# More unused transposes ahead of the first matrix unit of a planned attention and feed-forward kernel

## The chip, the cores and the metric

The kernel runs on one core of a Trainium2 chip. Its engines work side by side, each through its own list of instructions in order: TensorE (PE: matmuls, and PEld: the loads of their weights), VectorE (DVE), ScalarE (ACT), GpSimd (POOL), and SyncE (SP), whose list here holds the DMA issues. [...] The metric is the device time of one execution in microseconds (us); lower is better. The number given for a kernel is the median of its runs.

## The reference

Two blocks follow each other. The first is a causal linear attention with decay, in 4 batches x 8 heads, 768 tokens, 64 values per head; the second is a feed-forward block over the resulting 3072 x 512 matrix.

```python
for b in range(nb):                      # blocks of 64 tokens
    intra = np.einsum('bhic,bhjc->bhij', qb, kb) * Dmask[None]
    intra = np.einsum('bhij,bhjd->bhid', intra, vb)
    inter = np.einsum('bhid,bhde->bhie', qb * lam_pow[None], kv_state)
    out[:, :, sl] = intra + inter
    kv_state = lam_block * kv_state + np.einsum('bhsd,bhse->bhde', kb * rev_pow[None], vb)
x = out.transpose(0, 2, 1, 3).reshape(3072, 512)
h = x @ w_in                             # 512 x 2048, given as float64
result = np.maximum(0.01 * h, h) @ w_out # 2048 x 512, given as float64
```

## The kernel before

**Attention.** Tokens go in 24 chunks of 128 (two blocks of 64, all 8 heads at once). For a chunk c, SP loads k, q and v (`load_kq`, L338, two halves of four heads each; `load_v`, L388). PE transposes k and q in four steps each (`transposes`, L403, one pair of steps per half load), ACT copies the transposed tiles out of PSUM (L414 for k, L415 for q). PE multiplies in `scores` (L313, into the PSUM tile psc): the scores of the chunk, and the new part of the state from k and v. The k used for the state has been scaled by its decay on POOL (L419; on DVE in chunk 0), and q by its own (L423). DVE masks the scores (L452, giving "sc") and adds the state (L459); POOL decays the state (L462). `outputs` forms the chunk's output on PE (L313, into po): own, from sc and v, then the part that comes from the state, in two halves with a small copy (L491) between them. ACT and DVE split the output in three parts xh, xl, xm (L507, L508, L510), which the feed-forward block multiplies separately.

**Feed-forward block.** A group is four chunks, 512 tokens. A unit (`up`, L640) multiplies a group by 256 columns of w_in, in three products (xh with wh, xl with wl, xm with wm). The weights come as float64 (load L566), are turned into float32 by ACT and DVE (L578 to L585) and split in three (L591 or L593, L596, L602). The first unit needs chunks 0 to 3. Once all ups are through, `down` (L700) multiplies by w_out.

**The plan.** Nothing above is emitted directly. Class `Plan` collects every piece of work with an estimated duration on its engine (`add`), what it reads and writes, and a rank. `emit` runs a simple model of the engines, always taking the piece that can start earliest, and so gets an order in time, `timeline`. The instructions are then emitted in that order. While it emits, `emit` runs a second estimate: `soon` holds when each engine will be free and `over` when each piece ends; the start of a piece is the larger of the two, with an allowance per engine (`LAG`, and for a load the one in `SOON`) between a producer and its user. This second estimate serves one end only: where PE would be idle for more than 0.4 us, `self.idle(n)` puts in n unused transposes first. That is `busy` (L266): it transposes the identity into the PSUM tile b10. No one reads the result, and the transposes wait for nothing but the identity. Eleven of them (`WARM`) stand at the head of PE's list. From the first piece that writes b10 (the first unit) on, `idle` is None and no more are put in.

The prologue on PE therefore reads: eleven unused transposes, k0 and q0 (transposes of chunk 0), scores and state of chunk 0, k1, own0, q1, rest of the outputs of 0, scores of 1, q2, own1, k2, rest of 1, scores of 2, q3, k3, own2, q4, rest of 2, scores of 3, own3, q5, rest of 3, first unit, with unused transposes at nine places between.

Of the kernel before, what the change touches and what calls it, by code (L numbers as in the profile page):

```python
# [33 lines left out]
    return bass.AP(ap.tensor, ap.offset, a[:idx] + [[0, n]] + a[idx:])  # L34


class Plan:

    LAG = {"PE": 0.25, "ACT": 0.1, "DVE": 0.1, "POOL": 0.12, "DMA": 3.5}
    SOON = dict(LAG, DMA=2.0)

    def __init__(self):
        self.ops, self.last, self.rank = [], {}, 0.0
# [36 lines left out]
    def emit(self):  # L83
        n = len(self.ops)
        follows, heads = {}, {}
        for c in self.chains.values():
            m = [i for i in c if "PE" in self.ops[i][0]]
            for i in c[1:]:
                self.ops[m[0]][2].update(self.ops[i][2] - set(c))
            heads[m[0]] = m[1:]  # L90
            follows.update((i, m[0]) for i in m[1:])
        locked = []
        left = [len(o[2]) for o in self.ops]
        users = [[] for _ in range(n)]
        for i, o in enumerate(self.ops):
            for d in o[2]:
                users[d].append(i)
        free = dict(self.first)
        ends = [[] for _ in range(n)]
        able = {e: set() for e in free}  # L100
        for i, o in enumerate(self.ops):
            if not left[i]:
                for e in o[0]:
                    able[e].add(i)

        def since(i, e):
            return max((t + (0.0 if e == x != "DMA" else self.LAG[x]) for t, x in ends[i]), default=0.0)

        def good(i, e, t):
            ways = self.ops[i][0]  # L110
            return all(t + ways[e] <= max(free[x], t) + ways[x] + 0.3 for x in ways)

        done = []
        while len(done) < n:
            best = None
            for e in free:
                for i in able[e]:
                    if e == "PE" and (i != locked[0] if locked else i in follows):
                        continue
                    t = max(free[e], since(i, e))  # L120
                    if (best is None or (t, self.ops[i][3]) < best[:2]) and good(i, e, t):
                        best = (t, self.ops[i][3], i, e)
            t, _, i, e = best
            ways, fn = self.ops[i][:2]
            if i in heads:
                locked = list(heads[i])
            elif locked and i == locked[0]:
                locked.pop(0)
            for x in ways:
                able[x].discard(i)  # L130
            us = ways[e]
            if e == "PE" and t < self.cold:
                us *= 1.5
            elif e == "DVE" and fn is not None and free["POOL"] > t:
                us += 0.4 * min(free["POOL"] - t, us)
            free[e] = t + us
            done.append((t, len(done), i, e))
            for u in users[i]:
                ends[u].append((free[e] + self.more.get(i, 0.0), e))
                left[u] -= 1  # L140
                if not left[u]:
                    for x in self.ops[u][0]:
                        able[x].add(u)
        self.timeline = sorted(done)

        soon = dict.fromkeys(free, 0.0)
        soon.update(PE=self.warm, DVE=self.first["DVE"], DMA=self.first["DMA"])
        over = [(0.0, None)] * n
        for t, _, i, e in self.timeline:
            ways, fn, deps = self.ops[i][:3]  # L150
            t = max([soon[e]] + [over[d][0] + (0.0 if over[d][1] == e != "DMA" else self.SOON[over[d][1]]) for d in deps])
            if e == "PE":
                if self.spare in self.ops[i][4]:
                    self.idle = None
                if self.idle is not None and t > soon[e] + 0.4:
                    self.idle(int((t - soon[e] - 0.2) / 0.22))
            soon[e] = t + ways[e]
            over[i] = (soon[e], e)
            fn() if len(ways) == 1 else fn(e)
# [661 lines left out]
```

## Time and profile before

| | us |
|---|---|
| median of 3 runs | 610.2 (609.88 to 610.89) |
| the profiled execution | 609.84 |
| its span | 608.1 |
| PE busy | 597.1 (98%) |
| DVE busy | 313.2 (52%) |
| ACT busy | 267.9 (44%) |
| POOL busy | 85.6 (14%) |
| first unit starts (L640) | 30.98 |
| unused transposes (L266) | 35 in all, first at 1.4, last at 29.5 |

All times of the profile count from the start of the span. A row of the timeline gives the start, how long the group lasts, engine, line, operation, output tile and input tile, shape, and the number of instructions; in brackets stands how long the engine was idle ahead of it and what ended that idle time. In a row of the table of waits come the total, the number and the longest of the waits. Starts of PE and PEld differ little; PEld is the sharper of the two for short groups, since ends of matmuls are modelled. The line of tenths splits the span in 40 slices of 15.2 us.

### The profile page before, as it was taken

How to read it: one execution, taken by the hardware profiler on the slowest of the kernel's cores; microseconds unless marked ns; L12 is line 12 of the kernel's file. 1: busy time of each engine (PE TensorE's matmuls, PEld its weight loads, DVE VectorE, ACT ScalarE, POOL GpSimd, SP SyncE). 2: the span in 40 equal slices, each digit the busy share in tenths (PEclk: the TensorE clock that was granted, in tenths of full speed). 3: DMA queues.
4: the chain of work that ended last, by engine and by line, in shares of the span. 5: the costliest groups of instructions: out<-in, count | busy, mean ns of one | idle time of the engine just before them, and what ended most of it. 6: DMA issues, size and time to landing. Idle time of an engine off the chain costs nothing.

```text
span 608.1 us, 12940 instructions
## 1 busy us (share of the span) xinstructions
PE 597.1 (98%) x5391; PEld 494.0 (81%) x5391; DVE 313.2 (52%) x417; ACT 267.9 (44%) x428; POOL 85.6 (14%) x91
## 2 busy tenths in 40 slices
PE   8799999999999999999999999999999999999997
PEld 6578888888888888888788888888888888888886
DVE  5899872334253426226366755545454544635531
ACT  4778874333455656565577422222222313214111
POOL 1653331215133014104000000000000000000000
PEclk9999999999999999999999999999999999999999
DMA  9899864767788888886686843424334343433201
GB/s 218 214 281 256 244 182 119 180 143 186 188 219 243 215 239 200 226 249 215 227 288 232 279 141 106 171 74 143 131 103 138 109 136 109 134 104 123 85 1 69
DMA packets 147754, 105.18 MB, mean 173 GB/s; under 512 B 123632, under 2 KB 124400, under 8 KB 147696
## 3 DMA queue, kind: packets, MB, share of 16 engines
q1 hardware_dynamic: 147552, 104.36, 58.9%
q8 instruction: 42, 0.69, 0.5%
q14 instruction: 16, 0.13, 0.1%
q10 hardware_dynamic: 144, 0.00, 0.0%
HBM read 68.69 MB, written 35.65 MB: 172 GB/s over the span
## 4 chain that ended last, share of the span: by engine, by line
PE 94%; DMA 2%; SPq 1%; ACT 1%; DVE 1%; issue 0%; DVEq 0%; ACTq 0%
PE b L640 44%; PE b L700 18%; PE po L700 11%; PE psc L700 11%; PE po L313 4%; PE pt L700 4%; PE psc L313 3%; DMA raw<-in_moe_w_in_dram 2%; SPq L338 1%; PE po L403 0%; PE pt L403 0%; ACT low L580 0%; DVE w L584 0%; DVE w L585 0%; SPq L388 0%
## 5 line engine op out<-in xcount | busy, mean ns | idle before, releaser
L682 ACT ACTIVATE xh<-att 128x1024 fp32r<-128x1024 f32 x48 | 50.7, 1060 | 148.9 <-PE b L700 140.7
L683 DVE SCALAR_TENSOR_TENSOR xl<-att,xh 128x1024 fp32r<-128x1024 f32 x48 | 58.6, 1222 | 95.6 <-ACT xh L682 95.6
L640 PE MATMUL b<-xh,wh 128*128 128x512 f32 (+1 forms) x392 | 102.9, 386 | 0.7 <-ACT xh L507 0.7
L640 PE MATMUL b<-xm,wm 128*128 128x512 f32 (+1 forms) x392 | 103.5, 391 | 0.0
L640 PE MATMUL b<-xl,wl 128*128 128x512 f32 (+1 forms) x392 | 102.8, 386 | 0.0
L640 PEld LDWEIGHTS b<-xh,wh 128*128 128x128 f32 x392 | 72.5, 188 | 15.8 <-ACT xh L507 0.9
L640 PEld LDWEIGHTS b<-xl,wl 128*128 128x128 f32 x392 | 72.5, 188 | 14.8
L658 ACT ACTIVATE b<-b 128x512 f32<-128x512 f32 x96 | 56.0, 584 | 63.1 <-PE b L640 63.1
L640 PEld LDWEIGHTS b<-xm,wm 128*128 128x128 f32 x392 | 70.9, 188 | 15.2 <-ACT b L658 0.7
L661 ACT ACTIVATE gs<-b 128x512 f32<-128x512 f32 x96 | 56.7, 598 | 42.2 <-PE b L640 37.7
L700 PE MATMUL b<-wh,xh 128*128 128x512 f32 x192 | 74.7, 389 | 0.0
L700 PE MATMUL b<-wl,xl 128*128 128x512 f32 x192 | 74.7, 389 | 0.0
L685 DVE SCALAR_TENSOR_TENSOR xm<-xl,xh 128x1024 fp32r<-128x1024 f32 x48 | 58.7, 1226 | 4.7
L700 PEld LDWEIGHTS b<-wl,xl 128*128 128x128 f32 x192 | 36.1, 188 | 7.6
L700 PEld LDWEIGHTS b<-wh,xh 128*128 128x128 f32 x192 | 36.0, 187 | 7.5
L452 DVE TENSOR_TENSOR att<-psc,att 128x512 f32<-128x512 f32 x24 | 16.5, 689 | 45.7 <-PE psc L313 45.7
L423 POOL TENSOR_TENSOR att<-att 128x512 f32<-128x512 f32 (+1 forms) x21 | 26.3, 1251 | 96.9 <-DVE att L383 42.5
L419 POOL TENSOR_TENSOR att<-att 128x512 f32<-128x512 f32 (+1 forms) x23 | 28.5, 1239 | 65.3 <-DMA att<-in_k_dram 19.9
L700 PE MATMUL psc<-wh,xh 128*128 128x512 f32 x96 | 37.3, 389 | 0.0
L700 PE MATMUL psc<-wl,xl 128*128 128x512 f32 x96 | 37.3, 389 | 0.0
L700 PE MATMUL psc<-wm,xm 128*128 128x512 f32 x96 | 37.3, 389 | 0.0
L700 PE MATMUL po<-wh,xh 128*128 128x512 f32 x96 | 37.3, 389 | 0.0
(73 smaller groups left out, 790.0 us busy)
## 6 DMA issues: line engine op xcount, KB each, us to landing
att<-g SPq DMA_DIRECT2D x48, 512.0 KB, 3.3
g<-gs SPq DMA_DIRECT2D x47, 512.0 KB, 4.0
raw<-in_moe_w_in_dram SPq DMA_DIRECT2D x16, 512.0 KB, 5.6
raw<-in_moe_w_out_dram SPq DMA_DIRECT2D x16, 512.0 KB, 4.7
att<-in_k_dram SPq DMA_DIRECT2D x48, 128.0 KB, 4.1
att<-in_v_dram SPq DMA_DIRECT2D x24, 256.0 KB, 4.3
out_dram<-gs SPq DMA_DIRECT2D x23, 256.0 KB, 2.1
wo<-w SPq DMA_DIRECT2D x8, 512.0 KB, 5.7
```

Of the source, the lines that this page charges most:

```text
L313: nc.tensor.matmul(dst[HALF[cols]], lhsT=lhsT[HALF[rows]], rhs=rhs[HALF[rows]], start=start, stop=True, skip_group_check=True)
L338: nc.sync.dma_start(out=dst[:, z * HP:(z + 1) * HP, :], in_=y[z::2].rearrange("h p d -> p h d"))
L419: lambda e="POOL": ENG[e].tensor_tensor(kr[nr], kr[nr], _bc(pow_k, 3, D)[nr], op=ALU.mult), ["fk"], [f"k{i}"])
L423: add(eng, us, lambda: e.tensor_tensor(o, x, _bc(pow_q, 2, 2)[:, :, m, :], op=ALU.mult), ["fq", dep], [f"qsT{i}"])
L452: add("DVE", 0.69, lambda: nc.vector.tensor_tensor(sc, psc[:, :, lower, :], decay, op=ALU.mult), ["psc", "fk"], ["sc"])
L640: nc.tensor.matmul(dst, lhsT=w[z][:, kk * 2 * P + f * P:kk * 2 * P + (f + 1) * P], rhs=x[z][:, kk, toks], start=start and kk == 0, stop=kk ...
L658: add("ACT", ns, lambda b=b: nc.scalar.activation(out=b, in_=b, func=AF.Copy, bias=0.0, scale=S + 1.0), [], [kb], rank=-1.5)
L661: add("ACT", ns, lambda b=b, r=r: nc.scalar.activation(out=r, in_=b, func=AF.Prelu, bias=0.0, scale=1.0 / WS, alpha=0.01), [kb], [f"gs{jg} ...
L682: add("ACT", 1.05, lambda: nc.scalar.activation(out=h, in_=graw[j], func=AF.Copy, bias=0.0, scale=NEAR), reads, wr("h"))
L683: add("DVE", 1.25, lambda: nc.vector.scalar_tensor_tensor(l, graw[j], 1.0, h.bitcast(F32), op0=ALU.mult, op1=ALU.subtract), reads + [f"rh{ ...
L685: add("DVE", 1.25, lambda: nc.vector.scalar_tensor_tensor(m, l.bitcast(F32), -S, h.bitcast(F32), op0=ALU.mult, op1=ALU.add), [f"rh{j}", f" ...
L700: nc.tensor.matmul(acc[tb][z // 2][:, cols], lhsT=ring[j][z][:, f * T + tb * P:f * T + (tb + 1) * P], rhs=W[pp][z][:, f * d_model:(f + 1) ...
```

## The change

The second estimate gets another allowance for a load (2.6 in place of 2.0 us between the end of its issue and its use), and each unused transpose is counted at 0.16 in place of 0.22 us, so that more of them are put in an idle time of the same length. The allowance moves from the class into `emit`, which changes nothing else. The first estimate, which makes the order, is not touched.

```diff
     LAG = {"PE": 0.25, "ACT": 0.1, "DVE": 0.1, "POOL": 0.12, "DMA": 3.5}
-    SOON = dict(LAG, DMA=2.0)
...
         self.timeline = sorted(done)
 
+        SOON = dict(self.LAG, DMA=2.6)
         soon = dict.fromkeys(free, 0.0)
...
-            t = max([soon[e]] + [over[d][0] + (0.0 if over[d][1] == e != "DMA" else self.SOON[over[d][1]]) for d in deps])
+            t = max([soon[e]] + [over[d][0] + (0.0 if over[d][1] == e != "DMA" else SOON[over[d][1]]) for d in deps])
             if e == "PE":
...
                 if self.idle is not None and t > soon[e] + 0.4:
-                    self.idle(int((t - soon[e] - 0.2) / 0.22))
+                    self.idle(int((t - soon[e] - 0.2) / 0.16))
```

In the built program the eleven at the head stay, and the numbers of unused transposes further on become these; all other instructions of all engines keep their order:

| ahead of | before | after |
|---|---|---|
| q0 | 0 | 3 |
| scores of chunk 0 | 3 | 4 |
| state part of chunk 0 (second product into psc) | 3 | 1 |
| own0 | 1 | 2 |
| scores of chunk 1 | 2 | 4 |
| own1 | 3 | 4 |
| scores of chunk 2 | 1 | 5 |
| own2 | 4 | 3 |
| own3 | 6 | 9 |
| q5 | 0 | 4 |
| rest of the outputs of chunk 3 | 1 | 0 |
| sum | 24 | 39 |

## The prediction

> **What bounds the kernel now.** Four views, in this order: the page's tenths by slice, the table of waits of TensorE after 31 us, the timeline ahead of the first unit, the chain that ended last.
>
> ```profile
> PE   8799999999999999999999999999999999999997
> PEclk9999999999999999999999999999999999999999
> DMA  9899864767788888886686843424334343433201
> ```
>
> PE is full from the third slice (30.4 us) on; only the first two have room. The table of waits from 31 us to the end has two rows:
>
> ```profile
> PE b L640 <- ACT xh L507: 0.7, 1, 0.7
> PE po L313 <- ACT att L491: 0.3, 1, 0.3
> ```
>
> Behind the first unit PE waits 0.3 us in 577 us. So the time is the start of the first unit (L640, 30.98 us) plus a fixed PE stretch, and the change can act only through that 30.98. What sets it is at the end of the chain cut to 0 to 32 us:
>
> ```profile
> 20.82 6.54 DMA raw<-in_moe_w_in_dram
> ...
> 28.86 0.41 PE pt L403 x2
> 29.27 0.04 issue
> 29.31 0.45 PE pt L403 x2
> 29.76 0.02 issue
> 29.78 0.02 ACTq L415
> 29.80 0.04 issue
> 29.84 0.59 ACT att L415
> 30.42 0.51 ACT xh L507
> ```
>
> The transposes of q of chunk 5 (q5 below; k, q, v, sc and own are numbered by chunk) go in pairs, one pair behind each half load. The trace's landing events put the halves of q5 at 28.73 and 29.27 us; the second pair starts at 29.31. Copy L415, then xh L507, then the unit follow without a gap. The load sits in a queue in which SP issues without a pause over 0.1 us from 0.7 to 33 us, with DMA 0.8 to 0.9 busy. So loads set the start of the first unit, and PE runs ahead and waits, as its rows show:
>
> ```profile
> 6.04 0.66 PEld L266 LDWEIGHTS b<-att 128*128 128x128 f32 x3
> 7.75 0.31 PEld L266 LDWEIGHTS b<-att 128*128 128x128 f32 x3
> 13.08 1.16 PE L313 MATMUL psc<-att 64*64 64x64 f32 x64 [1.08 <-DVE att L459]
> 16.20 0.20 PEld L403 LDWEIGHTS b<-att 128*128 128x128 f32 x2 [0.32 <-DMA att<-in_k_dram]
> 18.48 1.16 PE L313 MATMUL psc<-att 64*64 64x64 f32 x64 [0.82 <-POOL att L419]
> 21.09 0.20 PEld L403 LDWEIGHTS b<-att 128*128 128x128 f32 x2 [0.45 <-DMA att<-in_k_dram]
> 27.46 0.93 PE L313 MATMUL po<-att 64*64 64x64 f32 x48 [1.09 <-DVE att L452]
> 28.83 0.20 PEld L403 LDWEIGHTS pt<-att 128*128 128x128 f32 x2 [0.59 <-ACT att L491]
> 29.31 0.20 PEld L403 LDWEIGHTS pt<-att 128*128 128x128 f32 x2 [0.28 <-DMA att<-in_q_dram]
> ```
>
> The first two rows give the price of one unused transpose: 0.66 / 3 = 0.22 us before the clock is granted (0.214 by the pitch of the first eleven), 0.31 / 3 = 0.103 after (0.107 in the longer group at 25.5). The trace's clock record grants at 6.68 us and never drops. A switch from these transposes to a 64-row matmul costs a further 0.17 (the idle "issue" in front of those groups).
>
> **The change, place by place.** The built program differs on PE alone; DVE, ACT, POOL and SP have the same instructions in the same order. The counts go from 3, 3, 1, 2, 3, 1, 4, 6, 1 to the following.
>
> - *Before q0: 0 to 3, before the clock.* The second pair of k0 starts at 4.60 and needs 2 x 0.214, to 5.03; three more end at 5.67. The halves of q0 landed at 5.14 and 5.72. First pair 5.67 in place of 5.18; second 5.67 + 0.43 = 6.10 in place of 5.76. Copy L415 and the first scores (7.13) wait for that second pair: +0.34. If each wait cost time as well, up to the full 0.64; two waits between full-height transposes already landed cost nothing at 10.60 us (four loads in 0.42), so 0.34.
> - *Before the first scores: 3 to 4.* Fill starts behind q0 at 6.53: one at 0.214, three at 0.107, 0.17 for the switch: 7.23, ahead of the copy at 7.47. Nothing.
> - *Before the second product of chunk 0: 3 to 1.* Here the row is packed (7.13 + 0.62 + 0.31 + 0.17 = 8.24 as seen), so -0.21. It waits too for v0 (landed 6.93) and k's factor (7.16), both earlier. Running delay +0.13 (up to +0.43).
> - *Before own0: 1 to 2.* Held by DVE's L452 (9.69 in before), PE ready at 8.86 + 0.42 + 0.21 + 0.17 = 9.66 against 9.75, shifted alike. Nothing; 0.1 if that cover went.
> - *Before the scores of chunk 1: 2 to 4.* 1.08 idle covers 0.21.
> - *Before own1: 3 to 4.* L452 ends at 14.99, PE starts at 15.09, and 14.56 + 0.36 + 0.17 is 15.09 as well: packed, +0.11. Running delay +0.24 (up to +0.54).
> - *k2, where it is lost.* PE is through with own1 at 15.88 and waits 0.32 for the halves of k2 (landed 16.16 and 16.52; pairs start 16.20 and 16.56). At +0.24 it is through at 16.12, still early. At +0.54 it starts at 16.46, second pair 16.66: 0.1 late. POOL's L419 and scores of chunk 2 keep their times.
> - *Before the scores of chunk 2: 1 to 5.* +0.43 under 0.82 idle, of which 0.17 is the switch: 0.65 is cover.
> - *Before own2: 4 to 3.* Packed behind k3, -0.11; given back at q4, whose second half lands at 23.05.
> - *Before own3: 6 to 9.* +0.32 under 1.09 idle (DVE: w's L602, L508, L452).
> - *Around q5: 0 to 4 ahead, 1 to 0 behind.* Own3's loads end at 28.25; four end at 28.68, the first half lands at 28.73. Nothing. Had own3 been late, the second pair has 0.38 more before 29.31 moves. The one removed lets the last outputs of chunk 3 go 0.11 earlier, but L507 stands 0.48 behind L415 on ACT, the same pitch as at 23.63 to 24.11: it is L415 that holds it. No gain.
>
> SP's queue holds loads that wait for PE: k2 (9.57 us) needs the second product of chunk 0, done at 8.93, +0.13 (up to +0.43) still ahead of SP's 9.47. Nothing behind it moves. DVE's work behind q2's copy (15.49) shifts by about 0.1 and meets at 18.85 what it waits for anyway.
>
> Sum: 0.00. Bounds: all three kinds of saving kept, -0.21 - 0.11 - 0.11 = -0.43; no cover anywhere, 3 x 0.214 + 12 x 0.107 = +1.93. I take 0, since each place has its cover in a row. The profiled execution is 609.84 (span 608.1 and 1.74 around it), 0.36 under the median of the runs shown; no change to it is no change to the median: 610.2.
>
> [...] Up to 6.68 us PE ran nothing but transposes (22 matmul rows, L266 and L403), and the pitch halved between 6.7 and 7.75: here transposes did earn the clock. [...]
>
> **Rivals.**
> 1. *The early delay gets past k2* (loads earlier against PE than in this execution). It goes through POOL's L419 to the scores of chunk 2, and k3 has only 0.56 more. At most +0.54 - 0.21 (own2 and behind) to +0.54: 610.5 to 610.7. For it: the packed rows at own1. Against: two load waits in a row.
> 2. *Slower: the fill is paid in full.* Place: every one of the ten. If PE and not the loads sets the pace from 4 us to the first unit, each transpose added moves it: +1.93, 612.1; it shows from 1.93 less half of the cover at own3 (1.09 - 0.17) and q5 (0.48), which is +1.23: 611.4. It decides where the idle rows of 0.32, 0.45, 1.09 and 0.59 are gone. For it: the costs in time are PE's own and certain, the covers belong to one execution. Against: DMA at 0.9 and SP without a pause.
> 3. *Faster: the fill holds the clock.* PE has the lowest share between 25.5 and 31 us (3.17 of 5.5 us busy). If executions outside the profile lose the clock there, the unit starts cold; eight of its matmuls take 2 us, so some 1.7 us at half clock go, and 13 transposes there instead of 7 prevent it: 608.5. If only the slower of the shown runs suffer, the gain is 0.4 (610.2 to 609.8). Against: no drop in the record, spread of runs only 609.88 to 610.89.
>
> **How the numbers follow.** A difference under 0.2% (1.2 us) is about what a measurement of this kernel cannot tell from none. Forecast 0.55 and rival 1 0.13 lie within it: 0.68. Rival 2: 0.20, slower. Rival 3: 0.12, faster. The range leaves out about half of rivals 2 and 3: 609.1 (between 608.5 and the lowest run) to 611.7 (half-way in rival 2). The forecast's own range is 609.8 to 610.8, the shown runs' spread.
>
> **What would show it.** Right: first unit at 31.0 +/- 0.15, q5's second pair within 0.05 of its landing, idle before scores of chunk 1, own3 and q5 shrunk by the fill's length, first scores at 7.4 to 7.8, k2's wait shorter by 0.2 to 0.5. Wrong: k2's pairs start with no wait left, SP's k2 load is issued late, or L640 starts later than 31.3 with PE packed before it; or the clock is granted at another time than 6.7 us.

## The result: slower by 0.27%, lost behind the start of the first unit

The changed kernel takes 611.64 us (median of 22 runs, 610.41 to 614.24), the kernel before 609.93 in the same comparison (22 runs, 609.38 to 612.91). The ratio is 1.0027, with a 95% interval of 1.0014 to 1.004. The forecast was no change, 610.2 us.

The profiled execution of the changed kernel has a span of 609.4 us, 1.4 more than before. Ahead of the first unit most things went as foretold. Its timeline, in the rows that answer to those shown of before (all line numbers stand one higher):

```profile
12.67 1.16 PE L314 MATMUL psc<-att 64*64 64x64 f32 x64 [0.85 <-DVE att L460]
16.28 0.20 PEld L404 LDWEIGHTS b<-att 128*128 128x128 f32 x2 [0.26 <-DMA att<-in_k_dram]
18.51 1.16 PE L314 MATMUL psc<-att 64*64 64x64 f32 x64 [0.33 <-POOL att L420]
20.69 0.20 PEld L404 LDWEIGHTS b<-att 128*128 128x128 f32 x2 [0.24 <-DMA att<-in_k_dram]
27.49 0.93 PE L314 MATMUL po<-att 64*64 64x64 f32 x48 [0.76 <-DVE att L453]
29.17 0.20 PEld L404 LDWEIGHTS pt<-att 128*128 128x128 f32 x2 [0.19 <-DMA att<-in_q_dram]
30.84 2.13 PE L641 MATMUL b<-xh,wh 128*128 128x512 f32 x8 [0.84 <-ACT xh L508]
```

The idle times ahead of the scores of chunks 1 and 2 and ahead of own3 have shrunk by about the length of the fill put into them (by 0.23, 0.49 and 0.33 us). q5's second pair still starts 0.04 us behind its landing (29.13), and the first unit starts at 30.84 instead of 30.98, in both kernels 1.71 us behind that landing. The time is lost later, where PE had no wait at all. PE's waits from 31 us on, in the changed kernel, have a row that before does not have:

```profile
PE po L314 <- issue: 1.4, 1, 1.4
PE b L641 <- ACT xh L508: 0.8, 1, 0.8
PE po L314 <- ACT att L492: 0.3, 1, 0.3
```

"Issue" is idle time for which the profile knows no releaser. Here is the place, in PE's timeline of the changed kernel, and the same place before:

```profile
54.48 1.11 PE L314 MATMUL psc<-att 64*64 64x64 f32 x64
55.41 0.41 PE L314 MATMUL po<-att 64*64 64x64 f32 x13
57.22 0.33 PE L314 MATMUL po<-att 64*64 64x64 f32 x3 [1.41 <-issue]
57.48 1.20 PE L641 MATMUL b<-xh,wh 128*128 128x512 f32 x4
```

```profile
54.66 1.11 PE L313 MATMUL psc<-att 64*64 64x64 f32 x64
55.59 0.41 PE L313 MATMUL po<-att 64*64 64x64 f32 x16
55.94 1.19 PE L640 MATMUL b<-xh,wh 128*128 128x512 f32 x4
```

PE stops after 13 of the last 16 small matmuls of chunk 6, in the middle of one loop without a single wait, and goes on 1.41 us later. The idle time of the row counts from the modelled end of the matmul ahead of the gap. Counted in starts from that of the first unit, PE is 0.04 us ahead of the kernel before up to the gap and 1.68 us behind it from there on, so the stall costs 1.72 us. A further 0.15 us is won near 223 us, and the first unit is 0.14 us earlier; together that is the 1.4 us.

A stop inside such a group points at the instructions themselves. The page counts them, in the queues of part 3 and the engines of part 1:

```profile
PE 598.5 (98%) x5406; PEld 495.5 (81%) x5406; DVE 312.4 (51%) x417; ACT 268.5 (44%) x428; POOL 86.4 (14%) x91
...
q8 instruction: 42, 0.69, 0.5%
```

The 42 packets on q8 hold 16,384 bytes each. PE has 2 x 5,406 instructions and some 50 that only signal, so 0.69 MB is, by estimate, some 64 bytes for each of them, and one packet 256 instructions of PE. Of the two kernels' seventh packets, that of before runs from 55.34 to 56.27 us and that of the changed kernel from 54.89 to 55.82. Counted from 0 in order of start, signals included, the matmul behind the gap is PE's record 1,985. In the kernel before, record 1,985 stands 30 instructions (15 transposes, each a weight load and a matmul) further on in the program, among the long matmuls of a unit, and starts at 58.36.

That gave the theory tested below. By it PE's program comes in blocks of 256 instructions, and the next block is brought by a packet while PE works on the present one. A round of a chunk is 272 instructions (8 transposes and 128 small matmuls, each with its weight load) in 3.3 us. Where a whole block falls in that stretch, PE is through with it in 2.5 us (record 1,729 at 53.31, 1,985 due at 55.8), sooner than the next has come; where the border lies among a unit's matmuls of 0.23 us each, PE takes longer (54.10 to 58.36 in before). Thirty instructions more moved the border from one to the other, and there it costs 1.72 us.

### The profile page after: what moved, and what is told of

The parts are those of the page before. It is cut to its first block, busy times and chain, and to the rows that moved or that the text cites. A ratio compares the mean times of both kernels' runs of the same rounds, so it can differ in the third digit from the quotient of the medians.

```text
span 609.4 us, 12970 instructions
## 1 busy us (share of the span) xinstructions
PE 598.5 (98%) x5406; PEld 495.5 (81%) x5406; DVE 312.4 (51%) x417; ACT 268.5 (44%) x428; POOL 86.4 (14%) x91
## 4 chain that ended last, share of the span: by engine, by line
PE 95%; DMA 2%; POOL 1%; DVE 1%; issue 0%; SPq 0%; ACT 0%; DVEq 0%; ACTq 0%
PE b L641 44%; PE b L701 18%; PE psc L701 11%; PE po L701 11%; PE po L314 4%; PE pt L701 4%; PE psc L314 3%; DMA att<-in_k_dram 1%; DMA att<-in_q_dram 1%; POOL att L420 1%; PE pt L404 1%; PE po L404 0%; SPq L339 0%; DVE wm L603 0%; PE b L404 0%
## 5 line engine op out<-in xcount | busy, mean ns | idle before, releaser
L585 DVE TENSOR_SCALAR w<-w 128x512 int32<-128x512 int32 x32 | 19.4, 605 | 36.9 <-ACT w L579 36.7
```

Of the source, the lines that this page charges most:

```text
L585: add("DVE", 0.42, lambda: nc.vector.tensor_scalar(d, d, 3, None, op0=ALU.logical_shift_left), [], [key])
```

## The experiments

The rivals were the fill itself (rivals 1 and 2 of the prediction), and an accident (a block late in one profile, tied to nothing). In the first two edits the fill has 15 or 40 unused small matmuls more ahead of own3, in the kernel before; in the third 25 more, in the changed kernel (there `n == 9`).

```diff
             nc.tensor.transpose(out=b1[0][:, 0:P], in_=ident, identity=ident)
+        for _ in range(15 if n == 6 else 0):
+            nc.tensor.matmul(b1[0][HALF[0], 0:D], lhsT=ident[HALF[0], 0:D], rhs=ident[HALF[0], 0:D], start=True, stop=True,
+                             skip_group_check=True)
```

**e1, the same number of instructions elsewhere.**

> The kernel before with its 24 unused transposes where they were, and 15 unused 64x64 matmuls (30 PE instructions with their weight loads, the same number as the 15 added transposes, some 0.26 us in all) in the idle time ahead of own3, where PE has 0.9 us to spare. Instruction-block theory: the border of the program block that PE stalled on in the changed kernel falls on the same instruction, so PE stands still for 1 to 1.8 us near 56 us with no wait, and the time is 1.0 to 1.7 us above before. Fill theory (the fill's own time, or its delay on the early chunks, costs): no change, first unit at 31.0, no stall. Accident theory (a late program block in one profile, not tied to the count): no stall, no change.

The size was wrong. Such a matmul of the identity runs as two pairs on PE (80 matmul records for 40), and one pair takes 0.059 us and not 0.0175: 60 instructions and 1.8 us. So the first unit started at 31.40, 0.42 late. Behind it came the stall, at record 1,985 again, though that is now another instruction, in the middle of the scores of the round:

```profile
55.05 1.11 PE L316 MATMUL psc<-att 64*64 64x64 f32 x62
57.06 0.21 PE L316 MATMUL psc<-att 64*64 64x64 f32 x1 [0.90 <-issue]
```

611.53 us, ratio 1.0033 (1.002 to 1.0047). The number of the record holds, and not the instruction. The stall is a little shorter than the 1 us or more foretold, and it does not need a block that falls whole in the dense stretch: PE had 4.9 us of work in the block ahead of this border (51.24 to 56.16), more than the kernel before has there (4.26). The packet was late by another way. It started 3.44 us after PE had entered that block, against 0.3 to 2.6 us in the other six stalls; why is not shown.

**e2 and e3, many more instructions.**

> The same with 40 unused 64x64 matmuls (80 PE instructions, some 0.7 us, still inside the 0.9 us ahead of own3). Instruction-block theory: the border now lies before the dense stretch of chunk 6, PE takes over 4 us from one border to the next there, so no stall near 56 us and a time within 0.5 us of before, although the most instructions were added. Fill theory: no change or slightly slower. Accident theory: no change.

> The changed kernel with all its 39 unused transposes and 25 unused 64x64 matmuls more ahead of own3 (40 pairs over before). Instruction-block theory: no stall near 56 us, 1.0 to 1.7 us faster than the changed kernel and within 0.5 us of before. Fill theory: as slow as the changed kernel or slower. Accident theory: anything the changed kernel shows.

For the same reason they put in 160 and 100 instructions and 4.7 and 2.95 us. Their first units start at 33.88 and 32.48 us, and that delay is in the time: 612.58 (ratio 1.0047, 1.0034 to 1.0059) and 611.2 (1.0018, 1.0009 to 1.0028). So neither kept within 0.5 us of before, as forecast for hidden fill. What they do tell: neither has a stall. PE's waits of e3 behind its first unit:

```profile
PE b L644 <- ACT xh L511: 0.8, 1, 0.8
PE po L317 <- ACT att L495: 0.3, 1, 0.3
```

From first unit to the end of the span, e2 takes 576.9 and e3 576.9 us; before takes 577.1, the changed kernel 578.6. The kernels with the most added instructions are free of the loss.

**e4 and e10, the changed kernel again.**

> The changed kernel itself, unaltered, once more. Instruction-block theory: the stall of 1 to 1.8 us near 56 us is there again, at the same instruction (after 13 of the last 16 small matmuls of chunk 6). Accident theory: no stall there, or one at another instruction.

> The changed kernel unaltered, beside it on the same chip. Instruction-block theory: the stall at the same instruction again, of 0.4 to 2.7 us; executions at a clock of 0.997 (one window of 3.4 us at half clock) now and then, none at 0.994.

611.64 us (ratio 1.0014, 0.9999 to 1.0029) and 611.73 (1.0032, 1.0016 to 1.0048). The stall stands at the same instruction in both, of 0.72 and 0.61 us (e4's shorter than foretold): no accident. e4 had its full clock from 6.74 us on, nearly as before (6.68), and so tells most about the early steps: its first scores start at 7.46 us; the prediction had 7.47.

**e6, the exact number, at other places.** 8 and 7 transposes more in the kernel before, in its two longest idle times, nothing else.

```diff
-        for _ in range(n):
+        calls.append(n)
+        for _ in range(n + {5: 8, 9: 7}.get(len(calls), 0)):
             nc.tensor.transpose(out=b1[0][:, 0:P], in_=ident, identity=ident)
```

> The kernel before with 15 more unused transposes in its two longest idle times alone (8 ahead of the scores of chunk 1, 7 ahead of own3), so that PE has exactly as many instructions ahead of chunk 6 as in the changed kernel, and none of the changed places. Instruction-block theory: first unit at 30.8 to 31.3, a stall of 0.7 to 1.6 us near 57 us after 13 of the last 16 small matmuls of chunk 6, time 0.8 to 1.6 us above before. Fill theory: no change, since idle time covers all 15.

First unit at 30.59 us, earlier than before, and:

```profile
55.34 0.41 PE L316 MATMUL po<-att 64*64 64x64 f32 x13
58.26 0.33 PE L316 MATMUL po<-att 64*64 64x64 f32 x3 [2.52 <-issue]
```

The same 13 of 16, with a stall longer than foretold. 611.47 us; over 12 runs the ratio is 1.0015 (0.9995 to 1.0034), so the time alone settles nothing, but its profile does: the place of the stall follows from the number of instructions.

**e7 and e8, the traffic ahead of the block.** One store of 512 KB at 48.4 us made twice (e7, shown), or left out (e8, with `if (g, p) != (0, 0)` ahead of it and another unit's result read back).

```diff
-            lambda: nc.sync.dma_start(out=G[g][p].rearrange("p (f t) -> p f t", f=2)[:, :, toks], in_=y),
...
+    def put():
+            for to in [G[g][p]] + [spare] * ((g, p) == (0, 0)):
+                nc.sync.dma_start(out=to.rearrange("p (f t) -> p f t", f=2)[:, :, toks], in_=y)
```

> The changed kernel, in which the result of the second unit (512 KB, stored at 48.4 us) is stored a second time to a place that nobody reads, right ahead of the late program block in the DMA queues. If the block is late because it stands behind data transfers: it lands later by what 512 KB take at 340 GB/s, some 1.5 us, and PE's stall grows from 1 to 1.4 us to 2 to 3 us. If the block's lateness has nothing to do with the load of the queues: the stall stays 0.9 to 1.4 us.

> The changed kernel without that store (the result of the second unit is left out; where it is read back, another unit's is read instead). If the block is late because it stands behind data transfers: it lands some 1.5 us earlier, the stall shrinks to under 0.5 us, and the time falls by 0.7 to 1.4 us. Otherwise the stall stays at 0.9 to 1.4 us.

With the store twice the stall was 2.38 us, without it 0.16:

```profile
57.93 0.47 PE L315 MATMUL po<-att 64*64 64x64 f32 x3 [2.38 <-issue]
```

```profile
56.34 0.33 PE L314 MATMUL po<-att 64*64 64x64 f32 x3 [0.16 <-issue]
```

613.83 us (1.0055, 1.0038 to 1.0072) and 611.34 (1.0022, 1.0003 to 1.0042); without the store, the six runs at full clock (below) have a median of 610.75, against 611.41 for the changed kernel. Both went as a block behind data transfers would, by some 0.7 to 1.0 us each (packet's end against 55.60, the mean of the changed kernel's three) rather than 1.5. One profile each is thin for that, since e6 shows a stall of 2.52 without an extra store. What settles the cause of the stall is the table of the seven profiles with a stall and of the kernel before. Times come from the seventh packet of q8 and from the matmul behind the gap, in us; idle is the profile's.

| kernel | packet ends | PE goes on | between | idle |
|---|---|---|---|---|
| changed | 55.82 | 57.22 | 1.40 | 1.41 |
| e1 | 55.62 | 57.06 | 1.44 | 0.90 |
| e4 | 55.60 | 56.94 | 1.34 | 0.72 |
| e6 | 56.78 | 58.26 | 1.48 | 2.52 |
| e7 | 56.57 | 57.93 | 1.36 | 2.38 |
| e8 | 54.90 | 56.34 | 1.44 | 0.16 |
| e10 | 55.37 | 56.69 | 1.32 | 0.61 |
| before | 56.27 | 58.36 | 2.09 | none |

The idle time varies by 2.4 us, the time from the packet's end to PE's next matmul only between 1.32 and 1.48. PE was waiting for that packet. In before PE gets to that record 0.7 us after the block would be there. The other borders say the same. If packet n brings the records from 193 + 256n on, the 13 profiles hold 535 borders, and PE passes none sooner than 1.23 us after its packet's end; eight lie under 1.5 us, and they are these seven stalls and one border inside own3 in e3, with 0.11 us of idle time. So PE stood still, for 0.16 to 2.52 us, where the profile shows no wait for a semaphore. What makes a packet late stays open: e7 and e8 point at the data transfers, without settling it.

**e5, the early fill kept, the late fill cut.** 15 transposes fewer in the changed kernel, where the idle time is longest.

```diff
-        for _ in range(n):
+        calls.append(n)
+        for _ in range(n - {6: 4, 10: 7, 11: 4}.get(len(calls), 0)):
             nc.tensor.transpose(out=b1[0][:, 0:P], in_=ident, identity=ident)
```

> The changed kernel with its early fill as changed (3, 4, 1, 2 ahead of q0 to own0; 4, 5, 3 ahead of own1, the scores of chunk 2 and own2), and 15 unused transposes fewer where the idle time is longest (scores of chunk 1: 0 instead of 4, own3: 2 instead of 9, q5: 0 instead of 4). PE then has as many instructions ahead of the first unit as before. Instruction-block theory: no stall near 56 us, first unit at 30.8 to 31.3, time within 0.5 us of before, 1 us or more under the changed kernel. Fill theory (the packed early places cost): still 0.5 us or more above before, with the first unit late.

No stall near the border, as expected. But 611.9 us (ratio 1.0013, 0.9994 to 1.0032), and the first unit at 32.27: neither theory had that. The windows of this profile (columns: stretch, its length, busy time of PE, PEld, DVE, ACT and POOL, then the granted clock, DMA share and GB/s) say why:

```profile
13.90:17.30 3.40, 3.40 (x71) 2.95 (x64) 2.48 (x5) 2.05 (x4) 0.62 (x1) 0.50 0.88 169
17.30:27.50 10.20, 8.08 (x262) 6.52 (x254) 9.06 (x13) 6.87 (x13) 7.55 (x6) 1.00 0.95 242
27.50:37.80 10.30, 8.77 (x83) 7.06 (x84) 9.80 (x15) 4.42 (x9) 5.33 (x6) 0.50 1.01 255
```

The clock fell to half for 3.4 us and again for 10.2 us. One run of twelve kept it throughout, and that one took 609.80; one such run says little about the early fill. The same shows in all runs by their mean granted clock, where a half-clock window of 3.41 us is worth some 0.003 (an estimate: half of 3.41 us in a span of some 610):

| kernel | runs | full (0.999 up) | one window (0.996 to 0.998) | two or more (below 0.996) | median of the full |
|---|---|---|---|---|---|
| before | 102 | 81 | 5 | 16 | 610.0 |
| changed, e4, e10 | 45 | 32 | 13 | 0 | 611.4 |
| e5 | 12 | 1 | 5 | 6 | 609.8 |
| e1 | 10 | 8 | 2 | 0 | 611.4 |
| e6 | 12 | 10 | 1 | 1 | 611.4 |
| e7 | 10 | 0 | 8 | 2 | none |
| e8 | 10 | 6 | 4 | 0 | 610.75 |
| e2 and e3 | 16 | 16 | 0 | 0 | see there |
| e9 and e11 | 24 | 24 | 0 | 0 | 609.9 |

So the fill does hold the clock: with 15 transposes fewer in the long gaps 11 of 12 runs lost it, before 21 of 102 (9 of the 35 beside e5), and the losses of two windows are gone in the changed kernel. One run of e6 (0.994) still has one, though e6 has 23 transposes in its two longest gaps and the changed kernel 13. The changed kernel's 13 losses of a single window probably have another place, the one that e7's profile shows, where the clock drops inside the stall, at 57.63 us:

```profile
53.00:57.60 4.60, 2.55 (x130) 2.24 (x129) 4.39 (x6) 2.88 (x7) 1.96 (x1) 1.00 1.04 398
57.60:61.00 3.40, 3.07 (x9) 2.43 (x9) 1.42 (x3) 2.56 (x5) 1.87 (x2) 0.50 1.07 292
```

No profile of the changed kernel itself caught this; that its one-window losses are the stall's rests on e7 and on the 40 runs of e2, e3, e9 and e11, whose profiles show no stall and which have no loss. Against it stands e8, with four such losses in ten runs and a stall of 0.16 us in its profile; how long the stall was in those four is not known.

**e9 and e11, the fill without the instructions.** The changed kernel's fill in its places, of about its length, from fewer and longer instructions.

```diff
-        for _ in range(n):
+        for w, m in ((4, n // 8), (2, n % 8 // 4)):
+            for _ in range(m):
+                nc.tensor.matmul(b1[0][:, 0:w * P], lhsT=ident, rhs=_bc(ident, 1, w), start=True, stop=True, skip_group_check=True)
+        for _ in range(n % 4):
             nc.tensor.transpose(out=b1[0][:, 0:P], in_=ident, identity=ident)
```

> The changed kernel with the same places and about the same length of fill, in fewer instructions: every eight unused transposes become one unused matmul with 512 columns (two pairs of weight load and matmul instead of eight), every four one with 256 columns. PE then has 7 pairs fewer than before ahead of chunk 6 instead of 15 more. Instruction-block theory: the border leaves the dense stretch on its other side, no stall near 57 us, first unit at 30.6 to 31.4, full-clock executions 1.0 to 1.6 us under the changed kernel and within 0.4 us of before. With the fill still holding the clock: no execution at a granted clock of 0.994 or less, and none of 0.997 either if those come from the stall. Fill theory: as slow as the changed kernel.

> The coarse fill of e9 once more, unaltered. Instruction-block theory with the fill holding the clock: no stall near 57 us, median 609.6 to 610.3, no execution at a granted clock below 0.999, while some one in six of the executions of before are at 0.996 or less; so its mean is a little under before's, its median the same. If e9's twelve executions were luck: some below 0.999 among these.

Record 1,985 now starts at 59.54 us, over 2 us behind its block, and the round runs through:

```profile
55.49 0.41 PE L317 MATMUL po<-att 64*64 64x64 f32 x16
55.83 1.19 PE L644 MATMUL b<-xh,wh 128*128 128x512 f32 x4
```

610.0 and 609.81 us against 610.08 and 610.26 for before beside them: ratios 0.999 (0.9976 to 1.0003) and 0.9988 (0.9975 to 1.0001). Against the changed kernel this is some 1.7 us. Against before the mean of all runs is 609.94 (24) to 610.51 (the 40 beside them, of which 7 lost their clock), while the runs at full clock differ by some 0.1 us in the median; each interval alone still touches 1.

## Why the prediction was wrong

**The step that failed** is in its first part: "Behind the first unit PE waits 0.3 us in 577 us. So the time is the start of the first unit (L640, 30.98 us) plus a fixed PE stretch, and the change can act only through that 30.98." The first unit moved by -0.14, +0.26 and +0.10 us in three profiles of the changed kernel. The stretch behind it was not fixed: it went from 577.1 to 578.6 us, because its borders of blocks lie where the number of instructions ahead of them puts them, and one now costs 1.72 us. The list of places counted the time of 15 transposes, and not that they are 30 instructions; the row that hints at this, q8 with its 42 packets, was on the page.

**The sum over the ten places** was right within what the landings of loads scatter, and so was its mechanism: in before and in all three profiles of the changed kernel the first unit starts 1.71 us behind the landing of q5's second half (29.27; 29.13, 29.53 and 29.37). Where the clock was granted as in before, the first scores came 0.01 us from the forecast (e4, 7.46). In the changed kernel's own profile the clock was granted at 4.98 us, one of the signs of being wrong; the first scores then start at 6.94 us and not at 7.4 to 7.8, since those transposes cost less than the 0.34 taken, and the first unit does not feel it. k2 took up the delay, but its wait shrank from 0.32 only to 0.26 us (0.23 in e4) and not by 0.2 to 0.5: own1 started 0.14 us later (0.21), and k2 itself landed 0.08 us later (0.12). The fill ahead of chunk 1, own3 and q5 was hidden, and SP's queue issued k2 at 9.62 us against 9.57.

**Rival 1** (the delay gets past k2) did not happen in any of the three, which all still wait for k2. **Rival 2** foretold a slower kernel of 611.4 to 612.1 us, and the median lies there, but by luck: it needed the first unit to be late by 1.2 us or more, and e6's profile has the stall with its first unit 0.39 us early. **Rival 3** had the right mechanism at the wrong weight. The clock falls in one run in five of before, and a run with two windows or more takes 613.0 us in the median against 610.0, so a loss costs more than the 1.7 us taken. Where it falls in before no profile caught; e5's shows it ahead of and at the first unit. With the longer fill none of 45 runs lost two windows or more, of before 16 of 102; one profile without a drop and three shown runs were too few to see them. In the change, the stall takes back more than this gives: +1.4 us in the runs at full clock (610.0 to 611.4), and, as it seems, new losses of the clock in the stall.

**The clock.** The prediction has transposes earn the clock in one profile, at 6.68 us, and rival 3 has them hold it. The runs agree: with the transposes cut in e5, 11 of 12 runs lost their clock, against 9 of the 35 of before beside them. How long a gap it takes is not shown: e5's first drop came with no gap over 1.44 us between the grant at 7.07 us and the drop at 13.90, and e7's came inside a single gap of 2.38 us, 2.1 us after it began.

**The chances:** 0.68 on a difference within 0.2% was too much for a kernel whose PE list had not been followed past the change.

## What to carry to other kernels

In this kernel 30 more instructions in PE's list, with their own time hidden, moved the later borders of its program blocks (record 1,985 from a unit's matmuls, 58.36 us, into a round's small ones, 57.22). In seven profiles in which that border fell in or behind such a stretch of many short instructions and the packet was late, PE stopped for 0.16 to 2.52 us, which shows as idle time put down to "issue" inside an unbroken group. So count instructions as well as microseconds, look at the instruction queue's packets and their borders, and fill idle time with few long instructions, as e9 and e11 do here (610.0 and 609.81 us). Judge filler that holds a clock by the granted clock over many runs and not by one profile.

## What was not expected of the hardware

- In the seven stalls PE resumed 1.32 to 1.48 us after the end of the packet that, by the estimate above, holds its next 256 instructions. From PE's first record of the block ahead to its first behind the border, the way took 2.67 (e8) to 5.81 us (e1) there, with the DMA engines near full (share 0.98 from 53.0 to 55.8 us in the changed kernel); the dense block of the changed kernel keeps PE busy for 2.5 us (53.31 to 55.8).
- The half-clock windows that profiles caught lasted 3.41 and 10.24 us (e5) and some 3.4 us (e7, 57.6 to 61.0), and one came after a stretch whose longest gap was 1.44 us (e5, PE busy for 5.4 of 6.9 us).
- An unused 64x64 matmul of the identity in float32 runs as two pairs, of 0.059 us each, all from and to the same half of the partitions; the kernel's own, which its code spreads over both halves, take some 0.015 to 0.018. That the placement makes the difference is not shown.
